# A recurrence with a router and experts on one core: w2 loaded into slots, in the order in which the first tiles need the experts

## The chip, the core and the metric

The kernel runs on one core of one Trainium2 chip. The metric is the device time of one launch in microseconds (us); lower is better. The engines are TensorE (PE, with PEld for its weight loads), VectorE (DVE), ScalarE (ACT), GpSimd (POOL) and SyncE (SP). Each works through its own queue in order. SP only issues transfers here, ACT and POOL issue some as well; all of them share 16 DMA engines.

## The reference

A gated linear recurrence over 4 x 8 heads of 768 steps and 48 channels gives 3072 rows of 384. A router takes two of eight experts for each row, and the row is the weighted sum of what these two compute.

```python
for t in range(S):
    state = alpha[:, :, t, :, None] * state + np.einsum('bhd,bhe->bhde', k[:, :, t], v[:, :, t])
    y[:, :, t] = np.einsum('bhd,bhde->bhe', q[:, :, t], state)
x = y.transpose(0, 2, 1, 3).reshape(B * S, H * D)            # 3072 x 384
noisy_logits = x @ w_gate + np.log1p(np.exp(x @ w_noise)) * noise
top2 = np.argpartition(-noisy_logits, 2, axis=1)[:, :2]      # two of 8 experts
top2_w = softmax over the two
for e in range(E):
    for k in range(2):
        mask = top2[:, k] == e
        h = np.maximum(x[mask] @ w1[e], 0.0)                 # 384 -> 1024
        out[mask] += top2_w[mask, k, None] * (h @ w2[e])     # 1024 -> 384
```

Everything is in float32. w1 and w2 are 8 x 1.5 MB each.

## The kernel before

The work has two stages, and one hand-written order (inside `tc.manual_schedule()`, from line 935) interleaves them on every engine.

**The recurrence** takes 24 chunks (NT) of 128 rows. `beside` is walked by n. Iteration n loads v of chunk n + 2 and alpha, k and q of chunk n + 4, updates the state, and then goes through a list of pieces in a fixed order: `alphas(n + 2)` (transposes on PE, then two scans on DVE, P_all and over, lines 286 and 292), `keys(n + 2)` (line 305 on POOL), `scores(n + 1)` and `give(n - 4)`, `queries(n + 2)` (q_P on DVE, line 314) and `masked(n + 1)` (line 333), router pieces, `turn_k`, `output(n)` (lines 210 and 214) and `turn_y(n - 1)`, which writes the rows to `x_rows` in DRAM. The transposes of one iteration share two PSUM buffers (`tp`). Three buffers (NIN) each hold the inputs alpha, k and q; they are tiles of their own (line 238), and their padding is set once on POOL.

**The router** works in units of three chunks (UC); there are 8 units (NU). `give(n - 4)`, four iterations after a unit's last chunk, calls `enter`, which ranks the unit's choices and queues six scatters of entries into `table` in DRAM (`put_some`, three per iteration, line 138), and `plan_tiles`, which lays out tiles of up to 128 rows of one expert. `GIVEN` says how many tiles are known after each unit. FULL = 23 tiles are planned from the first five units (u = 4, at n = 18), the other 32 from all eight (u = 7, at n = 27). For the units between, `plan_tiles` only copies. The plan has two columns per tile: the expert, and the tile's first row in `table`.

**The experts** take 51 tiles (ALWAYS), two per iteration from n = 23 (TILES_AT) on. Each has four steps (`tile_steps`): load w1 of tile i + 1, gather x of tile i + 2 and the first half of layer 1; its second half, then `combine(i - 1)`; transposes of tile i + 1 and the first half of layer 2; its second half, then `scale(i)` and `get_first(i)`. `load_tab(i + 4)` goes ahead of the first step: on SP for the first 23 tiles, on POOL for the others, waiting for the table entries of the units that the tile's plan knew. `get_first` gathers (on POOL) what an earlier tile wrote to the same output rows, `combine` adds on DVE, and a scatter on POOL puts the rows back. `get_first` waits for all scatters before it.

**w2** stays in SBUF, 98 KB per partition: `w2[:, e]` holds expert e. `load_w2(part)` loads a quarter of an expert (384 KB) on SP. The 32 quarters are spread over iterations 0 to 22, one or two each, in the order of the experts; layer 2 picks `w2[:, ds(e, 1)]` with a register that PE loads from the plan (line 793). w1 (1536 KB) is loaded per tile into two buffers, by a register that SP loads (line 746).

Of the kernel before, what the change touches and what calls it, by code (L numbers as in the profile page):

```python
# [9 lines left out]
F32 = mybir.dt.float32  # L10
U32 = mybir.dt.uint32
I32 = mybir.dt.int32
AF = mybir.ActivationFunctionType
ALU = mybir.AluOpType
# [4 lines left out]
def kernel(  # L19
# [26 lines left out]

    nc = tc.nc
    B, H, S, D = q.shape  # L50
    N, DM = out.shape
    E, _, F = moe_w1.shape
    C = 128
# [17 lines left out]
    TROWS = E * RMAX + (E + 0) * C  # L71
    NONE = 2 * N
    RANGE = 1e-18
    FULL = (2 * UT * (NU - 3) - E * (C - 1) + C - 1) // C
    GIVEN = [0] * (NU - 4) + [FULL, FULL, FULL, NTILE]

    def pool(name, bufs, on=ctx, **kw):
        return on.enter_context(tc.tile_pool(name=name, bufs=bufs, **kw))
# [104 lines left out]
    def turn_noise(by_chunk, on):  # L183
# [2 lines left out]
            nc.tensor.transpose(tp[:, e, :], by_chunk[:, e, :], ident[0:NT, 0:NT])  # L186
        nc.scalar.copy(noise.rearrange("p n e -> p e n"), tp)

    W2_PARTS = 4
    w2 = const.tile([C, E, FO, DM], F32, name="w2")  # L190

    def load_w2(part):
        e, f = divmod(part, W2_PARTS)
        fs = ds(f * FO // W2_PARTS, FO // W2_PARTS)
        nc.sync.dma_start(out=w2[:, e, fs], in_=moe_w2[e].rearrange("(a p) d -> p a d", p=C)[:, fs, :])


    def few(on, shape, name):
# [36 lines left out]

    def fast_gla(on):
        one, two = on["one"], on["two"]
        ins = {x: [one.tile([C, H, DP], F32, name=f"{x}_in{i}") for i in range(NIN)] for x in "akq"}
        for x in "akq":
            for t in ins[x]:  # L240
                nc.gpsimd.memset(t[:, :, D:DP], 1.0 if x == "a" else 0.0)
# [397 lines left out]
        del to_put[:n]  # L639


    plan = const.tile([C, NTILE, 2], I32, name="plan")
    given = const.tile([C, NTILE, EV], F32, name="given")
    so_far = [const.tile([C, EV], F32, name=f"so_far{i}") for i in range(2)]
    again = const.tile([1, 1], F32, name="again")
# [1 line left out]
    more = const.tile([1, 1], F32, name="more")  # L647
    more_i = const.tile([1, 1], I32, name="more_i")
    tiles_i = const.tile([1, 1], I32, name="tiles_i")

    def plan_tiles(u, on):
        rp = on["one"]
# [36 lines left out]
        def of_expert(dst, at, shape):  # L689
# [12 lines left out]
        nc.vector.tensor_scalar(out=start, in0=start, scalar1=0.0, scalar2=None, op0=ALU.max)  # L702
        nc.vector.tensor_tensor(start, start, ready, op=ALU.min)
        nc.vector.tensor_tensor(so_far[now % 2], start, old, op=ALU.add)

        behind = rp.tile([C, K_MAX, EV], F32, name="behind")[:, 0:K]
        nc.vector.tensor_tensor(behind, number, ends[:, None, :].to_broadcast(shape), op=ALU.is_ge)
# [5 lines left out]
        nc.vector.scalar_tensor_tensor(row, em, float(C), region[:, None, :].to_broadcast(shape), op0=ALU.mult,  # L713
                                       op1=ALU.add)
        nc.vector.tensor_mul(row, row, behind)
        first = rp.tile([C, K_MAX], F32, name="first")[:, 0:K]
        nc.vector.reduce_sum(out=first, in_=row, axis=mybir.AxisListType.X)
        nc.vector.tensor_scalar(out=plan[:, lo:hi, 1], in0=first, scalar1=float(TROWS - C), scalar2=None, op0=ALU.min)
# [4 lines left out]
    def experts(on):  # L723
# [10 lines left out]
        def load_tab(i, units):  # L734
            if i >= NTILE:
                return
            by, engine = (nc.sync, mybir.EngineType.SP) if i < FULL else (nc.gpsimd, mybir.EngineType.Pool)
            r = nc.values_load(plan[0:1, i, 1:2], engines=[engine], min_val=0, max_val=TROWS - C,
                               skip_runtime_bounds_check_because=WHY)
            tabs[i] = on["tab"].tile([C, 8], F32, name="tab")  # L740
            take_tile(by.dma_start(out=tabs[i][:, 0:4], in_=table.bitcast(F32)[ds(r, C), :]), units)
# [48 lines left out]
        def layer2(i, part):  # L790
            o = os_[i]
            if part == 0:
                o["e"] = nc.values_load(plan[0:1, i, 0:1], engines=[mybir.EngineType.PE], min_val=0, max_val=E - 1,
                                        skip_runtime_bounds_check_because=WHY)
                o["ps"] = on["o"].tile([C, DM], F32, name="o_ps")
            for f in range(FO // 2):
                fo = part * FO // 2 + f
                nc.tensor.matmul(o["ps"], o["h"][part][:, f, :],  # L798
                                 w2[:, ds(o["e"], 1), fo, :].rearrange("p o d -> p (o d)"),
                                 start=fo == 0, stop=fo == FO - 1)  # L800

# [106 lines left out]
    with ExitStack() as es:  # L910
# [9 lines left out]
        def steps_of(i, n):  # L920
            units = NU if n >= NT + 4 else unit_of[i] + 1
            limit = min(ALWAYS, GIVEN[units - 1])
            steps = tile_steps(i, do, (units, limit), i >= ALWAYS - 2)
            if i + 4 < limit:
                steps[0] = lambda go=steps[0]: (load_tab(i + 4, unit_of[i + 4] + 1), go())
            return steps


        TILES_AT = 23
        W2_ITERATIONS = 23  # L930
        held = []
        beside = [[] for n in range(TILES_AT)] + [list(range(i, min(i + 2, ALWAYS))) for i in range(0, ALWAYS, 2)]
        assert 2 * (NT + 4 - TILES_AT) + 4 <= FULL
# [1 line left out]
        with tc.manual_schedule():  # L935
            load(0)
            load_v(0)
            load(1)
            for n in range(2):
                alphas(n)  # L940
                keys(n)
                queries(n)
                load(n + 2) if n == 0 else (load_v(1), load(3))
            held.append(load_router(on))
            scores(0)
            masked(0)
            turn_k(0)
            for n, tiles in enumerate(beside):
                work = [step for i in tiles for step in steps_of(i, n)]
                w2_at = [E * W2_PARTS * min(i, W2_ITERATIONS) // W2_ITERATIONS for i in (n, n + 1)]  # L950
                w2_parts = lambda: [load_w2(i) for i in range(*w2_at)]
                chunk = [lambda: (load_v(n + 2), load(n + 4), state(n)), lambda: alphas(n + 2),
                         lambda: (keys(n + 2), choose_part(n - 2, 0), choose_part(n - 3, 2)),
                         lambda: (scores(n + 1), give(n - 4)), lambda: (queries(n + 2), masked(n + 1)),
                         lambda: (choose_part(n - 2, 1), choose_part(n - 3, 3), route(n - 1), w2_parts()),
                         lambda: turn_k(n + 1), lambda: output(n), lambda: turn_y(n - 1)]
                last = [lambda: put_some(UC)]
                if n == 1:
                    last.append(lambda: clear_table(on["two"]))
                if n == 2:  # L960
                    chunk.insert(1, lambda: turn_noise(held.pop(), on))
                if n == NT + 1:
                    chunk.insert(0, lambda: out_of_range(0))
                    last.append(lambda: out_of_range(1))

                some = range(4)
                if n == TILES_AT - 3:
                    last.append(lambda: [load_tab(i, unit_of[i] + 1) for i in some])
                if n == TILES_AT - 2:
                    chunk.insert(3, lambda: (load_w1(0), [gather_x(i, unit_of[i] + 1) for i in some[:2]]))  # L970
                if n == TILES_AT - 1:
                    chunk.append(lambda: turn_x(0))
                chunk += last
                done = 0
                for j in range(len(work)):
                    work[j]()
                    upto_j = len(chunk) * (j + 1) // len(work)
                    for piece in chunk[done:upto_j]:
                        piece()
                    done = upto_j  # L980
                for piece in chunk[done:]:
                    piece()
# [3 lines left out]
    with tc.If(any_more > 0):  # L986
# [3 lines left out]
                              skip_runtime_bounds_check_because="a count of at most 2 C rows")  # L990
        with tc.If(redo > 0):
            taken.clear()
            again_by_levels()


# [28 lines left out]
```

## Time and profile before

| | |
|---|---|
| time, three runs | 778.04 us median (776.23 to 783.17) |
| profiled run | 777.69 us, span of the trace 776.1 us, mean clock 0.991 |
| PE, matmuls | 744.0 us busy, 96% of the span |
| PEld | 613.3 us, 79% |
| DVE / ACT / POOL | 264.6 / 197.3 / 296.8 us |
| moved by DMA | 141.77 MB, 183 GB/s over the span |
| layer 1 (line 786), layer 2 (line 798) | 282.7 and 273.7 us of PE |
| chain that ended last | PE 71%, DVE 16%, issue 6%, DMA 3%, POOL 2% |

"Issue" is time in which an engine waited for nothing that the profile shows. Matmuls are pipelined and their ends are modelled, so that a busy PE need not be one at its peak. The profile's slices are a fortieth of the span, 19.4 us, and their digits tenths of busy time; PEclk is the clock that PE was granted. A wait is put down to the engine whose signal came last by the profile, and "x8" after an operation says how many instructions a line stands for. Idle time of an engine that doesn't bound anything costs nothing.

### The profile page before, as it was taken

Reading aid. Unit: us, or ns where it says so; the run is one execution under the profiler, and the core shown is the slowest. Engines: PE = TensorE matmul, PEld = TensorE weight load, DVE = VectorE, ACT = ScalarE, POOL = GpSimd, SP = SyncE. Lnnn points to the kernel's source line nnn. Section 1 sums busy time; section 2 is a strip of 40 time slices with the busy share of each in tenths; the row PEclk is TensorE's granted clock in tenths of the full one; section 3 lists DMA queues with packets and bytes.
Section 4 is the critical chain, followed back from the end, with each engine's and each line's share of the span. In section 5 each row is a group of like instructions: output and inputs, shape, how many; then the busy total and the mean of one; then the engine's idle time right before and its main releaser. Section 6 shows DMA issues by size and latency. Waiting matters only on the chain.

```text
span 776.1 us, 14314 instructions
## 1 busy us (share of the span) xinstructions
PE 744.0 (96%) x5239; PEld 613.3 (79%) x5239; DVE 264.6 (34%) x860; ACT 197.3 (25%) x381; POOL 296.8 (38%) x416
## 2 busy tenths in 40 slices
PE   5999999989899999989999999999999999999995
PEld 3988888878687888767788777887788877888774
DVE  6678998998302122301111111111111111111110
ACT  2456466545211221111111111111111111111110
POOL 4234666756523331333332333333333333333221
PEclk9999999999999999999999999999999999999998
DMA  9899999986834845365754565445544555455530
GB/s 152 156 217 197 186 199 189 206 190 180 266 106 161 268 159 186 109 210 154 252 187 190 213 219 181 156 176 196 189 174 149 203 205 210 169 177 214 208 123 23
DMA packets 149026, 141.77 MB, mean 183 GB/s; under 512 B 111725, under 2 KB 123599, under 8 KB 148948
## 3 DMA queue, kind: packets, MB, share of 16 engines
q1 hardware_dynamic: 135712, 116.45, 52.9%
q0 software_dynamic: 12224, 23.78, 9.4%
q8 instruction: 45, 0.74, 0.4%
q10 hardware_dynamic: 1012, 0.53, 0.3%
q14 instruction: 33, 0.27, 0.1%
HBM read 131.95 MB, written 15.25 MB: 190 GB/s over the span
## 4 chain that ended last, share of the span: by engine, by line
PE 71%; DVE 16%; issue 6%; DMA 3%; POOL 2%; ACT 0%; ACTq 0%; DVEq 0%; POOLq 0%
PE h_ps L786 31%; PE o_ps L798 30%; DVE over L292 3%; DVE P_all L286 3%; PE x_ps L775 2%; DVE MT L333 2%; PE tp L275 1%; PE o_ps L354 1%; DVE q_P L314 1%; PE y L214 1%; DMA prev<-out_dram,where 1%; PE sc L328 1%; PE y L210 1%; DMA x_in<-x_rows,where 1%; DMA out_dram<-prev,where 1%
## 5 line engine op out<-in xcount | busy, mean ns | idle before, releaser
L786 PEld LDWEIGHTS h_ps<-xt,w 128*128 128x128 f32 x2448 | 280.9, 192 | 15.7 <-DVE prev L819 3.1
L786 PE MATMUL h_ps<-xt,w 128*128 128x128 f32 x2448 | 282.7, 275 | 2.7 <-DVE prev L819 1.9
L798 PE MATMUL o_ps<-w,h 128*128 x816 | 273.7, 489 | 0.0
L798 PEld LDWEIGHTS o_ps<-w,h 128*128 128x128 f32 x816 | 151.7, 191 | 95.7 <-issue 2.1
L823 POOL DMA_INDIRECT out_dram<-prev,where x51 | 52.1, 1022 | 183.4 <-DVE prev L819 164.6
L788 ACT ACTIVATE h<-h_ps 128x512 f32<-128x512 f32 x102 | 61.0, 598 | 228.4 <-PE h_ps L786 220.5
L819 DVE SCALAR_TENSOR_TENSOR prev<-prev,tab,o 128x384 f32<-128x384 f32 x49 | 30.3, 618 | 256.7 <-DMA prev<-out_dram,where 144.3
L805 POOL DMA_INDIRECT prev<-out_dram,where x51 | 52.3, 1025 | 123.1 <-DMA out_dram<-prev,where 117.7
L777 DVE COPY xt<-x_ps 128x384 f32<-128x384 f32 x51 | 28.4, 557 | 181.4 <-PE x_ps L775 179.7
L814 ACT ACTIVATE o<-o_ps,tab 128x384 f32<-128x384 f32 x49 | 28.5, 581 | 234.7 <-PE o_ps L798 229.9
L766 POOL DMA_INDIRECT x_in<-x_rows,where x51 | 52.5, 1029 | 60.7 <-issue 45.5
L138 POOL DMA_INDIRECT table<-entry,place_u x48 | 50.5, 1051 | 13.4 <-issue 11.8
L305 POOL TENSOR_TENSOR k_P<-k_P,over 128x512 f32<-128x512 f32 x24 | 28.4, 1185 | 45.9 <-DVE over L292 32.7
L286 DVE TENSOR_TENSOR_SCAN P_all<-a_all,least 128x516 f32<-128x516 f32 x24 | 32.0, 1334 | 10.6 <-ACT a_all L283 5.2
L359 POOL TENSOR_TENSOR S<-S,end 128x384 f32<-128x384 f32 x20 | 22.7, 1135 | 32.7 <-DVE S L357 32.5
L292 DVE TENSOR_TENSOR_SCAN over<-a_all,P_all 128x515 f32<-128x515 f32 x24 | 34.1, 1421 | 0.8
L333 DVE COPY_PREDICATED MT<-upto,sc 128x512 f32<-128x512 uint32 x48 | 32.2, 723 | 1.3 <-PE sc L328 1.3
L328 PE MATMUL sc<-q_P,k_P 48*128 48x128 f32 x384 | 30.5, 297 | 1.2 <-DVE MT L333 0.9
L328 PEld LDWEIGHTS sc<-q_P,k_P 48*128 48x128 f32 x384 | 25.4, 198 | 5.9 <-issue 5.1
L775 PE MATMUL x_ps<-ident,x_in 128*128 128x128 f32 x153 | 25.1, 273 | 3.0 <-DMA x_in<-x_rows,where 3.0
L214 PE MATMUL y<-MT,vt 128*48 128x128 f32 x384 | 27.4, 287 | 0.0
L210 PE MATMUL y<-q_P,S 128*128 128x128 f32 x192 | 27.2, 287 | 0.0
(148 smaller groups left out, 600.8 us busy)
## 6 DMA issues: line engine op xcount, KB each, us to landing
w<-in_moe_w_dram SPq DMA_DIRECT2D x51, 1536.0 KB
w<-in_moe_w_dram SPq DMA_DIRECT2D x32, 384.0 KB
a_in<-in_alpha_dram SPq DMA_DIRECT2D x24, 192.0 KB
k_in<-in_k_dram SPq DMA_DIRECT2D x24, 192.0 KB
q_in<-in_q_dram SPq DMA_DIRECT2D x24, 192.0 KB
vt<-in_v_dram SPq DMA_DIRECT2D x24, 192.0 KB
x_rows<-y_sb SPq DMA_DIRECT2D x24, 192.0 KB
x_in<-x_rows,where POOLq DMA_INDIRECT x51
```

What stands on the lines that cost most here:

```text
L138: put = nc.gpsimd.indirect_dma_start(out=table, out_offset=bass.IndirectOffsetOnAxis(ap=place, axis=0), in_=entry, in_offset=None, bounds_ ...
L286: nc.vector.tensor_tensor_scan(P_all[:, 0:NP * CB], a_all[:, 0:NP * CB], least.rearrange("p j t -> p (j t)"), 0.0, op0=ALU.mult, op1=ALU.max)
L292: nc.vector.tensor_tensor_scan(over.rearrange("p j t -> p (j t)")[:, :0:-1], a_all[:, :1:-1], P_all[:, :1:-1], 0.0, op0=ALU.mult, op1=ALU.max)
L328: nc.tensor.matmul(c["sc"][i][:, j, :], c["k"][r, j, :], c["q"][r, j, :], start=True, stop=True)
L333: nc.vector.copy_predicated(MTs[n % 2][:, i], mask_upto, sc)
L766: nc.gpsimd.indirect_dma_start(out=x_in[i % NB], out_offset=None, in_=x_rows[0:units * UT, :], in_offset=bass.IndirectOffsetOnAxis(ap=wher ...
L775: nc.tensor.transpose(x_ps[:, a, :], x_in[i % NB][:, ds(a * C, C)], ident)
L786: nc.tensor.matmul(h_ps[:, fo, :], w1[:, a, ds((part * FO // 2 + fo) * C, C)], xt[:, a, :], start=a == 0, stop=a == KO - 1)
L788: nc.scalar.activation(os_[i]["h"][part], h_ps, AF.Relu)
L798: nc.tensor.matmul(o["ps"], o["h"][part][:, f, :], w2[:, ds(o["e"], 1), fo, :].rearrange("p o d -> p (o d)"), start=fo == 0, stop=fo == FO ...
L805: get = nc.gpsimd.indirect_dma_start(out=prev[i % 2].bitcast(U32), out_offset=None, in_=out.bitcast(U32), in_offset=bass.IndirectOffsetOnA ...
L823: put = nc.gpsimd.indirect_dma_start(out=out, out_offset=bass.IndirectOffsetOnAxis(ap=where[:, 0:1], axis=0), in_=rows, in_offset=None, bo ...
```

## The change

There are five parts.

1. w2 becomes eight slots. Slot k holds the k-th expert of those that the first batch of tiles uses (in the order of their number, and the unused ones behind them). `order_slots`, new, works this out on DVE right after the first plan; `expert_in` says which expert is in a slot, `slot_of` where an expert is. `load_w2` reads `expert_in` into an SP register for every quarter, and the plan gets a third column, the slot, which PE's register takes in layer 2.
2. The first batch is planned from four units: FULL is 17, planned at u = 3 (n = 15), and the second batch, at n = 27, has 38 tiles.
3. The w2 loads start at n = 16: one quarter at each of n = 16 to 19, four at 20, four at 21, one at 22 (after the router pieces, as before), and then two after the second and two after the fourth step of each tile, until all 32 are out: 19 quarters in tiles 0 to 4.
4. Tile i is declared free of the loads of slots behind i (up to i = 6), since the tiles before it use at most one new slot each.
5. The nine input tiles of alpha, k and q lie in the last one and a half slots of w2 instead of tiles of their own.

`load_tab` still issues on SP for tiles 0 to 22 (ALWAYS - 28 = 23).

```diff
-    FULL = (2 * UT * (NU - 3) - E * (C - 1) + C - 1) // C
-    GIVEN = [0] * (NU - 4) + [FULL, FULL, FULL, NTILE]
+    FULL = (2 * UT * (NU - 4) - E * (C - 1) + C - 1) // C
+    GIVEN = [0] * (NU - 5) + [FULL, FULL, FULL, FULL, NTILE]
...
     def load_w2(part):
-        e, f = divmod(part, W2_PARTS)
+        k, f = divmod(part, W2_PARTS)
         fs = ds(f * FO // W2_PARTS, FO // W2_PARTS)
-        nc.sync.dma_start(out=w2[:, e, fs], in_=moe_w2[e].rearrange("(a p) d -> p a d", p=C)[:, fs, :])
+        e = nc.values_load(expert_in[0:1, k:k + 1], engines=[mybir.EngineType.SP], min_val=0, max_val=E - 1,
+                           skip_runtime_bounds_check_because="a permutation of the experts")
+        put = nc.sync.dma_start(out=w2[:, k, fs],
+                                in_=moe_w2[ds(e, 1)].rearrange("o (a p) d -> p (o a) d", p=C)[:, fs, :])
+        for take in w2_takes:
+            tc.declare_no_dep(put.ins, take, reason="a slot behind those that the tile may take")
+        w2_loads[k].append(put.ins)
+
+    def take_w2(i, take):
+        for loads in w2_loads[i + 1:] if i < E - 1 else []:
...
-        ins = {x: [one.tile([C, H, DP], F32, name=f"{x}_in{i}") for i in range(NIN)] for x in "akq"}
+        places = w2.rearrange("p e f d -> p (e f d)").rearrange("p (n h d) -> p n h d", h=H, d=DP)
+        ins = {x: [places[:, E * FO * DM // (H * DP) - 1 - i - NIN * "akq".index(x)] for i in range(NIN)] for x in "akq"}
...
+    def order_slots(tiles, rp):
+        used = rp.tile([C, E], F32, name="used")
+        nc.vector.tensor_scalar(out=used, in0=tiles[:, 0:E], scalar1=1.0, scalar2=None, op0=ALU.min)
+        upto_it = rp.tile([C, E], F32, name="upto_it")
+        nc.vector.tensor_tensor_scan(upto_it, ones[:, 0:E], used, 0.0, op0=ALU.mult, op1=ALU.add)
+        nc.vector.memset(slot_of, 0.0)
+        nc.vector.tensor_tensor(slot_of[:, 0:E], upto_it, used, op=ALU.subtract)
...
+        nc.vector.tensor_copy(out=expert_in, in_=used)
...
+        if u is not None and not lo:
+            order_slots(so_far[now % 2], rp)
...
+        nc.vector.tensor_tensor(slots, behind, slot_of[:, None, :].to_broadcast(shape), op=ALU.mult)
+        slot = rp.tile([C, K_MAX], F32, name="slot")[:, 0:K]
+        nc.vector.reduce_sum(out=slot, in_=slots, axis=mybir.AxisListType.X)
+        nc.vector.tensor_copy(out=plan[:, lo:hi, 2], in_=slot)
...
-            by, engine = (nc.sync, mybir.EngineType.SP) if i < FULL else (nc.gpsimd, mybir.EngineType.Pool)
+            by, engine = (nc.sync, mybir.EngineType.SP) if i < ALWAYS - 28 else (nc.gpsimd, mybir.EngineType.Pool)
...
-                o["e"] = nc.values_load(plan[0:1, i, 0:1], engines=[mybir.EngineType.PE], min_val=0, max_val=E - 1,
+                o["e"] = nc.values_load(plan[0:1, i, 2:3], engines=[mybir.EngineType.PE], min_val=0, max_val=E - 1,
...
+            for at in (1, 3):
+                steps[at] = lambda go=steps[at]: (go(), more_w2(2))
...
-        W2_ITERATIONS = 23
+        w2_beside = {TILES_AT - n: parts for n, parts in ((7, 1), (6, 1), (5, 1), (4, 1), (3, 4), (2, 4), (1, 1))}
+        w2_parts = iter(range(E * W2_PARTS))
...
-                         lambda: (choose_part(n - 2, 1), choose_part(n - 3, 3), route(n - 1), w2_parts()),
+                         lambda: (choose_part(n - 2, 1), choose_part(n - 3, 3), route(n - 1), more_w2(w2_beside.get(n, 0))),
```

Left out: seven more instructions of `order_slots`, the column count of the plan, and lines for a general path that this input doesn't take.

## The prediction

> **What bounds the kernel now.** I read the page's slices first, then table of stretches, waits, timelines. The slices (19.4 us each) show two stages: ten with VectorE (DVE) and the DMA engines full, then thirty in which only TensorE (PE) is.
>
> ```profile
> PE   5999999989899999989999999999999999999995
> DVE  6678998998302122301111111111111111111110
> PEclk9999999999999999999999999999999999999998
> DMA  9899999986834845365754565445544555455530
> ```
>
> The same by stretches: us, busy time of PE, weight loads, DVE, ACT, POOL, then clock, DMA share, GB/s.
>
> ```profile
> 20.00:190.00 170.00, 162.99 (x1655) 147.06 (x1655) 146.75 (x350) 92.45 (x201) 92.19 (x145) 0.99 0.92 189
> 190.00:255.00 65.00, 61.48 (x423) 50.90 (x422) 17.07 (x81) 14.51 (x28) 26.91 (x35) 0.97 0.58 183
> 255.00:345.00 90.00, 86.88 (x517) 68.16 (x516) 23.38 (x118) 16.65 (x28) 28.28 (x32) 0.98 0.53 182
> 345.00:740.00 395.00, 395.00 (x2455) 318.69 (x2454) 60.92 (x289) 64.67 (x110) 133.58 (x142) 1.00 0.54 191
> ```
>
> In the recurrence (20 to 190 us) DMA is 0.92 busy, but PE is idle for only 7.0 us of 170; from 190 to 345 it is idle 6.6 us, from 345 to 740 not at all. A tile of the experts is a fixed 10.85 us (h_ps from 431.08 to 441.93). All that a change off PE can win before the tail is about 14 us of idle time, plus what the clock lost.
>
> In the chain of waits one full iteration of the recurrence on PE, back to back, is scores 1.09, q transposes 0.59, logits 0.80, turned keys 0.48, y 0.89 and 1.01, turned y 0.59, state 0.87, a and k transposes 0.87: 7.19 us. The P_all scans on DVE start at 66.12, 74.21, 82.12, 89.99, 97.88 and so on to 156.46, 169.38, 178.24, 185.03: 118.9 us for 15 iterations. PE's own share is 15 x 7.19, less 2 x (0.87 + 0.48) for chunks without a state: 105.2. The excess is 13.7, of which 12.92 - 7.19 = 5.7 is the iteration that plans tiles (n = 18). Here is what it does on DVE, and what PE does meanwhile and later:
>
> ```profile
> 159.76 0.98 DVE L629 SCALAR_TENSOR_TENSOR place_u<-at_f,place_f 128x6 uint32<-128x6 f32 x1
> 160.68 0.15 DVE L667 COPY total_sb<-h_ps 128x8 f32<-128x8 f32 x1
> 166.92 0.26 DVE L720 TENSOR_SCALAR given<-given 128x207 f32<-128x207 f32 x1
> 167.09 0.68 DVE L314 TENSOR_TENSOR q_P<-tp,P_all 128x512 f32<-128x512 f32 x1
> ```
>
> ```profile
> 159.55 1.07 PE L232 MATMUL h_ps<-w_r,yT 128*128 128x16 f32 x8 [1.07 <-DVE picked L622]
> 161.12 1.91 PE L210 MATMUL y<-q_P,S 128*128 128x128 f32 x8
> 336.83 0.55 PE L775 MATMUL x_ps<-ident,x_in 128*128 128x128 f32 x3 [2.99 <-DMA x_in<-x_rows,where]
> 337.35 7.12 PE L798 MATMUL o_ps<-w,h 128*128 x16
> ```
>
> The plan holds q_P back from 160.7 to 167.1. After a short PE idle y takes 1.91 instead of 1.06 us and o_ps 7.12 instead of 5.33: windows of 1 us show the granted clock at 0.50 from 161 to 164 and from 195 to 198. The one later stall, 2.99 us, follows the second plan (DVE 306.5 to 314.1).
>
> Does DMA bound anything? The SyncE (SP) queue in mid-recurrence:
>
> ```profile
> 120.31 1.25 SPq L163 DMA_DIRECT2D a_in<-in_alpha_dram  x1
> 121.61 5.20 SPq L163 DMA_DIRECT2D k_in<-in_k_dram  x1
> 126.85 1.00 SPq L163 DMA_DIRECT2D q_in<-in_q_dram  x1
> 127.89 1.16 SPq L195 DMA_DIRECT2D w<-in_moe_w_dram  x1
> ```
>
> PE's waits for it up to 190 us (total, times, longest):
>
> ```profile
> PE tp L275 <- DMA a_in<-in_alpha_dram: 5.4, 2, 4.2
> ```
>
> SP issues without a pause from 76 to 165 us, and one issue takes up to 5.20 us where the quick ones take 0.4[...]. Yet of the 5.4 us that PE waited for a_in, 4.2 is the first load, before any w2. The rest is 1.2, and DVE waits 1.68 before P_all at 178.24 with no cause named, perhaps q_in. The loads run four chunks ahead, so full rings cost almost nothing yet.
>
> **What the Trainium skill says.** "DMA: Bandwidth & Descriptors", section "Issuing engines are not separate DMA queues": all issuers run on the same 16 engines and interleave. The trace agrees: in the tiles the gather of prev (issued 203.22) lands at 212.06, in and ahead of a burst of w1. "TensorE: Matmul & The Clock Gate", Part 1: PE's clock halves after an idle window of about 3.4 us and stays so for at least one. The half rates seen here last about 3.4 us; that about 1 us of idle is enough is this trace's, not the page's.
>
> **The change part by part.**
>
> *Removed from the recurrence:* w2's 32 loads of 384 KB, 1.4 per iteration up to n = 22. Now 13 go out at n = 16 to 22 (8 of them at 20 and 21, where no a, k or q is loaded any more), 19 beside tiles 0 to 4. Gain: the 1.2 and 1.68 us of waits, 2.9. Bounds: 0 (those waits have other causes) and 8.0 (all of 13.7 - 5.7 is lost to DMA). I take 2.9.
>
> *Added to DVE at n = 15:* order_slots, 13 small instructions and a memset. Small dependent ones start 0.20 apart (161.64, 161.84, 162.06, 162.26): 13 x 0.20 + 0.06 = 2.7 us. The plan moves from n = 18 to 15 with 17 tiles for 23: 153 elements for 207 are 54/0.96 = 0.056 us less (the slope of 0.38 at 207 and 0.46 at 288 is 0.0010 per element) in 11 instructions, -0.6. Three new ones (slots, slot, the plan's third column): 0.32 + 0.32 + 0.18 = 0.8. Net 2.7 - 0.6 + 0.8 = 2.9. It stands before q_P and masked on DVE; PE's turned y waits for q_P's PSUM buffer, and next iteration's P_all and POOL's k_P follow. DVE is busy 146.75 of 170, PE 162.99: no slack to absorb it, so 2.9 in full. Bounds: 1 (slack of the two lighter iterations, 16 and 17) and 2.9 + 1.7 (another half-clock window of 3.4 us).
>
> *Second plan (n = 27):* 38 tiles for 32. 54 elements more in 11 instructions is +0.6, three new at 342 elements 0.52 + 0.52 + 0.18: +1.8 together. In the chain behind it (x_in, put, prev, table puts, x_in again at 329.32, landing before 336.83) everything shifts, so the 2.99 us stall becomes 4.8. I take 1.8; bounds 0 and 3.5 (a second half-clock window).
>
> *Moved to the tiles:* 4 x 384 KB per tile, beside w1's 1536 KB, so twice the bytes. A w1 burst takes about 4 us (568 to 573, up to 414 GB/s); w2's will take as much. Bursts of two w1 already occur (207 to 216, 230 to 238, 254 to 262) and only the first ends in a PE idle, 1.90 us at 212.87. SP holds w2 behind w1(i+1), and w1(i+2) behind it: 8 of 10.85 us. w1(3), issued 229.87, is needed at 238.55, and w1(4), issued 232.89, at 250.93, so 4 us more hidden. Slot loads: slot 3 is complete in tile 0, 4 in tile 1, ..., each three tiles before a tile can wait for it. Cost -1.9 (that idle disappears) to +10 (rival C), taken 0.5.
>
> *SP:* each w2 load gets a register load. Four tab issues with theirs took 3.27 us, 0.8 each, so four w2 loads are 3 to 4 us of a 7 us iteration at n = 20 and 21; x_rows (n - 1) and the four tab loads are behind them, then w1(0) at 188.85, needed at 199.82: hidden. expert_in is ready at n = 15, so n = 16 doesn't wait. *load_tab* keeps its first 23 on SP; 17 to 22 now wait for the last table puts (350.25), with w1(14) behind them: about 355 to 359, needed at 366.0. 0, bounds 0 and 3. *Inputs inside w2* and the third plan column read by PE: same instructions, nothing.
>
> Sum: -2.9 + 2.9 + 1.8 + 0.5 = +2.3. The profiled span 776.1 becomes 778.4. Its run took 777.69, close to the median 778.04 of 776.23 to 783.17; so 780.3, said as 780.
>
> **Rivals.**
>
> A, above: 780, own range 776 to 786.
>
> B, DMA was the hidden bound: SP's unbroken queue speaks for it, the short waits for a_in against. Then all 8.0 of excess go, with the 1.90 at 212.87, the 0.92 idle at 192 and its half-clock (1.7): -12.5, +2.9 + 1.8: -7.8, 770 (765 to 774).
>
> C, ends slower: the chain put, prev, combine falls behind in tiles 0 to 4. get_first(i) waits on POOL for the put before to land, then combine waits on DVE for prev, and xt of the tile after next stands behind combine. With one w1 burst per tile the chain's cycle, when catching up, is 8.4 us (prev at 360.98, 369.28, 377.69). If w2's burst adds its whole 3.9 us it is 12.3, over 10.85: 1.5 late per tile, 7 after five, met at n = 27 by the longer plan: 7 + 1.7 of clock + 2.3 - 0.5, about +10.5, so 789 (785 to 795). It decides from 10.85 us on. Against it: the double bursts above.
>
> D, the change doesn't do what it says: the input tiles, now part of w2, make loads wait for each other or slots for inputs. Price, if each chunk's three loads land one after another at 2 us each, some 4 us in part of 20 iterations: +20 and more, 800. Against: three w2 loads left in 1.6 us at 189 to 192 into one tile without waiting.
>
> **How the numbers follow.** A 0.53, B 0.20, C 0.22, D 0.05. The predicted time is A's. Under 1%, 7.8 us, a measurement of this kernel can hardly tell from no change (its own runs spread 6.9). Faster by over 1% is below 770.3: 0.14, all from B. Slower, above 785.8: most of C (0.18), D 0.05, A's end 0.03: 0.26. Within: 0.60. The range 769 to 792 leaves out some of B's and C's ends (0.06 and 0.07) and D.
>
> **What would show it.** DVE at n = 15 some 9 us between place_u and q_P, none at n = 18 (plan right). P_all iterations at n = 6 to 13 still 7.0 to 8.2 us with DMA well below 0.9: A; all near 7.2: B. SP issues near 0.4 us and pauses in SP's queue. Tiles 0 to 5 at 10.85 us plus recurrence work: A; growing idle before h_ps with prev or x_in as releaser: C. PE idle near 337 of 4.8 us. Wrong altogether if PE's own time per tile or iteration changed, or SP waited on w2.

## The result, and the profile after

The changed kernel takes 787.25 us (median of four runs, 786.08 to 789.54) against 778.04 before: a ratio of 1.0114 with an interval of 1.0069 to 1.0160, so it is slower by about 1%. The profiled span grew from 776.1 to 784.4 us, by 8.3, and the mean clock fell from 0.991 to 0.984.

The slices of the page after (19.6 us each) show the same two stages. New are a dip of PE and of its clock in the eighth slice, and DMA that is less full before that slice and fuller behind it.

```profile
PE   5999999799989999989999999999999999999995
DVE  6779999879411121510111111111111111111110
PEclk9999999699999999999999999999999999999998
DMA  9777678388979765446665544555544555445530
```

The stretches after, as before: us, busy time of PE, weight loads, DVE, ACT, POOL, then clock, DMA share, GB/s.

```profile
20.00:190.00 170.00, 161.52 (x1606) 145.76 (x1606) 146.16 (x350) 90.87 (x198) 89.25 (x143) 0.96 0.73 136
190.00:255.00 65.00, 60.45 (x424) 50.05 (x425) 21.03 (x94) 14.16 (x29) 24.59 (x32) 0.97 0.87 295
255.00:345.00 90.00, 85.97 (x532) 69.61 (x531) 23.96 (x114) 17.08 (x29) 31.07 (x35) 0.98 0.58 186
345.00:740.00 395.00, 394.03 (x2427) 316.51 (x2426) 61.78 (x296) 64.51 (x109) 135.05 (x144) 1.00 0.54 191
```

The transfers did move: in the recurrence the DMA share fell from 0.92 to 0.73, and in the next 65 us it rose from 0.58 to 0.87. PE didn't profit. In the recurrence it is busy 1.5 us less out of 170, at a clock of 0.96 where it was 0.99.

The loss can be located from the start of the scores on PE in each iteration. The intervals between these starts, in the same order before and after, are:

```
n = 6 to 13  before  8.10 7.32 7.91 8.45 6.29 7.19 8.04 7.19
             after   8.14 7.32 7.91 8.46 6.29 7.19 8.04 7.18
n = 14 to 21 before  7.91  8.45  6.29 7.20 12.50 7.70 8.03 7.75
             after   7.30 15.86 11.12 7.19  7.74 7.19 7.29 7.96
```

Interval n runs from the scores issued in iteration n to those of n + 1. The plan stands behind the scores of its iteration: it makes the 12.50 of before (n = 18) and the 15.86 of after (n = 15). This is the sum, by the starts of scores, of the first half of layer 1 of each tile, and of the end:

| us later (+) or earlier (-) than before | |
|---|---|
| first scores and the two intervals behind them | -1.1 |
| three iterations without a plan (7.91, 7.70, 8.03 become 7.30, 7.19, 7.29) | -1.9 |
| the plan's own iteration: +7.41 at n = 15, -4.76 at n = 18 | +2.65 |
| the iteration behind the plan at n = 15: 6.29 becomes 11.12 | +4.83 |
| the last interval, 7.75 becomes 7.96 | +0.2 |
| tile 0: 13.05 becomes 13.82; tile 4: 10.85 becomes 12.10 | +2.0 |
| tiles 9 to 11, the second plan: 10.95, 11.06, 16.08 become 11.20, 13.89, 14.01 | +1.0 |
| other tiles and the end | +0.6 |
| sum | +8.3 |

DVE in the plan's iteration after, cut to the ends of its three parts. `used` opens `order_slots`, `expert_in` closes it, q_P is what waits.

```profile
136.64 0.98 DVE L648 SCALAR_TENSOR_TENSOR place_u<-at_f,place_f 128x6 uint32<-128x6 f32 x1
...
141.42 0.17 DVE L673 TENSOR_SCALAR used<-so_far 128x8 f32<-128x8 f32 x1
...
143.76 0.17 DVE L690 CAST expert_in<-used 128x8 int32<-128x8 f32 x1
...
146.79 0.68 DVE L333 TENSOR_TENSOR q_P<-tp,P_all 128x512 f32<-128x512 f32 x1
```

From total_sb (137.56) to q_P the plan holds DVE for 9.2 us where it held it for 6.4. `order_slots` takes 2.42 us of it (141.42 to 143.84).

PE in the same stretch and later, each line with its idle time in brackets:

```profile
136.42 1.07 PE L249 MATMUL h_ps<-w_r,yT 128*128 128x16 f32 x8 [1.62 <-DVE picked L641]
...
148.25 2.58 PE L347 MATMUL sc<-q_P,k_P 48*128 48x128 f32 x16 [3.55 <-DVE MT L352]
...
153.24 2.05 PE L227 MATMUL y<-q_P,S 128*128 128x128 f32 x8
...
218.34 2.92 PE L834 MATMUL h_ps<-xt,w 128*128 128x128 f32 x24 [2.71 <-DMA w<-in_moe_w_dram]
...
338.10 7.25 PE L834 MATMUL h_ps<-xt,w 128*128 128x128 f32 x48 [2.78 <-DVE xt L825]
346.33 0.55 PE L823 MATMUL x_ps<-ident,x_in 128*128 128x128 f32 x3 [0.97 <-DMA x_in<-x_rows,where]
```

PE stops for 3.55 us ahead of the scores of iteration 16: they wait for DVE, where q_P and the masking MT stand behind the plan. These scores then take 2.58 us instead of 1.09, and the y behind them 2.05 instead of 1.06. That is the clock. The windows of this stretch (columns as in the stretches above) show it at half speed for the 10 us after the stop, with PE busy all the time; in the third window DMA moves almost nothing:

```profile
142.00:148.70 6.70, 2.43 (x19) 1.88 (x17) 6.22 (x26) 3.87 (x8) 0.04 (x1) 0.98 0.82 145
148.70:152.00 3.30, 3.30 (x22) 3.02 (x21) 3.23 (x6) 0.00 (x0) 1.68 (x1) 0.50 0.48 125
152.00:158.70 6.70, 6.70 (x39) 6.07 (x39) 3.52 (x16) 1.21 (x3) 4.98 (x7) 0.51 0.02 1
158.70:164.00 5.30, 5.30 (x60) 4.81 (x60) 4.29 (x6) 3.94 (x9) 1.49 (x4) 1.00 0.56 122
```

A shorter stretch at half speed, 3.41 us behind the ranking's stop, lies in the plan's iteration of both kernels (160.72 to 164.13 before, 138.15 to 141.56 after), so it doesn't count in the difference.

SP's queue is no longer continuous: here it pauses from 120.68 to 123.97. The issues of alpha and k, which took 1.25 and 5.20 us in the lines shown of before, take 0.71 and 1.11.

```profile
117.64 0.71 SPq L164 DMA_DIRECT2D w<-in_alpha_dram  x1
118.41 1.11 SPq L164 DMA_DIRECT2D w<-in_k_dram  x1
119.56 1.12 SPq L164 DMA_DIRECT2D w<-in_q_dram  x1
123.97 0.34 SPq L244 DMA_DIRECT2D x_rows<-y_sb  x1
```

### The profile page after: what moved, and what is told of

It reads as the page before. It is cut to its first block, busy times and chain, and to the rows that moved or that the text cites. A ratio compares the mean times of both kernels' runs of the same rounds, so it can differ in the third digit from the quotient of the medians.

```text
span 784.4 us, 14445 instructions
## 1 busy us (share of the span) xinstructions
PE 747.8 (95%) x5239; PEld 617.5 (79%) x5239; DVE 270.0 (34%) x878; ACT 196.8 (25%) x381; POOL 297.3 (38%) x416
## 4 chain that ended last, share of the span: by engine, by line
PE 71%; DVE 14%; issue 6%; DMA 5%; POOL 2%; ACT 1%; ACTq 0%; SPq 0%; POOLq 0%; DVEq 0%
PE h_ps L834 30%; PE o_ps L846 28%; DVE over L311 3%; DMA w<-in_moe_w_dram 3%; DVE P_all L305 2%; PE tp L294 2%; PE x_ps L823 2%; PE y L231 2%; PE sc L347 2%; DVE MT L352 2%; PE y L227 1%; PE o_ps L373 1%; PE h_ps L249 1%; PE tp L241 1%; DMA out_dram<-prev,where 1%
## 5 line engine op out<-in xcount | busy, mean ns | idle before, releaser
L139 POOL DMA_INDIRECT table<-entry,place_u x48 | 52.1, 1086 | 13.4 <-issue 11.6
L294 PE MATMUL tp<-ident,w 128*128 128x128 f32 x288 | 46.1, 298 | 7.2 <-DMA w<-in_alpha_dram 5.3
L294 PEld LDWEIGHTS tp<-ident,w 128*128 128x128 f32 x288 | 35.5, 156 | 11.8 <-POOL w L260 4.2
L311 DVE TENSOR_TENSOR_SCAN over<-a_all,P_all 128x515 f32<-128x515 f32 x24 | 36.4, 1517 | 0.8
```

The costliest lines, as they stand in the source:

```text
L139: put = nc.gpsimd.indirect_dma_start(out=table, out_offset=bass.IndirectOffsetOnAxis(ap=place, axis=0), in_=entry, in_offset=None, bounds_ ...
L294: nc.tensor.transpose(tp[:, j, :], src[:, 2 * j:2 * j + 2, :], ident)
L311: nc.vector.tensor_tensor_scan(over.rearrange("p j t -> p (j t)")[:, :0:-1], a_all[:, :1:-1], P_all[:, :1:-1], 0.0, op0=ALU.mult, op1=ALU.max)
```

## The experiments

All are timed in five rounds against the kernel before on the same chip. There were four sets, and the kernel before is not equally fast in them: 785.4 us in the first (e1 to e4), 777.1 in the second (e0, e5, e6, e7), 785.3 in the third (e8, e9), 783.8 in the fourth (e10, e11). The chip alone doesn't decide it: the second and the fourth set ran on the same one. So only ratios, and times within a set, are compared. "After" and "before" are the two kernels of the study.

**e0: the changed kernel again**

> The changed kernel as it is, beside the kernel before on the same chip as the other runs of this set: ratio 1.007 to 1.016, and in its trace the 9 us plan at n = 15 with the half clock behind it.

Measured: 786.02 us against 777.07, ratio 1.0128 (1.0098 to 1.0159). The plan's iteration and the next are 15.86 and 11.12 us, as in the first trace. Tiles 0 and 4 are not as there: 12.37 and 11.62 us, together 0.1 us over the kernel before, where the first trace has 2.0. That row of the table above isn't steady.

**e1: the order of the slots left out**

```diff
+    nc.vector.memset(slot_of, 0.0)
+    nc.vector.tensor_copy(out=slot_of[:, 0:E], in_=expert_ids)
+    nc.vector.tensor_copy(out=expert_in, in_=expert_ids)
...
-        if u is not None and not lo:
-            order_slots(so_far[now % 2], rp)
```

The slots are fixed by the experts' numbers at the start; for this input that is the order which `order_slots` would find.

> The changed kernel without order_slots: slot k holds expert k, set once at the start (for these inputs the first 17 tiles use experts 0 to 6 in the order of their number, so it is the same order). Theory H (the plan at n = 15 holds q_P and masked on DVE, PE runs idle, and its clock halves for 10 us): 2.4 us of DVE less, the 3.55 us idle of PE before the scores shrinks to about 1, the half clock at n = 16 to one window of 3.4 us or none: 5 to 7 us less than the changed kernel, 780 to 782 us. Theory L (the w2 loads beside the tiles are the loss: w1 and prev land late): at most the 2.4 us, about 785 us, and the waits for w1 in tiles 1 and 5 stay.

Measured: 787.92 us, ratio 1.0017 (0.9995 to 1.0038). Its trace has 13.31 and 10.11 for the plan's iteration and the next: shorter by 2.55 and 1.0 than in the first trace of after, and by 2.0 and nothing than in e10's (15.32 and 10.10), which is the same kernel as after. So 2.4 us of small DVE work left out shorten the plan's iteration by about as much. The half clock was expected to shrink to 3.4 us or to none; it lasts 6.8 us, as long as in e10 (0.50 from 152 to 158).

**e2: the kernel before with the early plan alone**

```diff
-    FULL = (2 * UT * (NU - 3) - E * (C - 1) + C - 1) // C
-    GIVEN = [0] * (NU - 4) + [FULL, FULL, FULL, NTILE]
+    FULL = (2 * UT * (NU - 4) - E * (C - 1) + C - 1) // C
+    GIVEN = [0] * (NU - 5) + [FULL, FULL, FULL, FULL, NTILE]
```

> The kernel before with one part of the change alone: the first batch of 17 tiles planned from four units at n = 15, the second of 38 at n = 27; w2 and inputs as before. Theory H: the hold is about 5.5 us instead of 6.4, so the first plan costs no more than at n = 18; the longer second plan adds about 0.5: 777 to 779 us. If the place n = 15 itself costs (it is followed by two iterations without slack), 781 to 783. Theory L: as before, 778.

Measured: 783.69 us, ratio 0.9976 (0.9956 to 0.9996). To plan at n = 15 instead of 18, without `order_slots` and with w2 loaded as before, costs nothing in this set. (Not shown in the edit: `load_tab` keeps its first 23 on SP, and two scratch tiles share a place.) In its trace PE waits 1.88 us for k_in at 135.43, ahead of the plan; the iterations are 10.16 and 13.59, and the one behind the plan is 6.29.

**e3: the w2 loads alone**

The fixed slots of e1, and the plan of before (five units, 23 tiles, at n = 18); the w2 loads as in the changed kernel.

```diff
-    FULL = (2 * UT * (NU - 4) - E * (C - 1) + C - 1) // C
-    GIVEN = [0] * (NU - 5) + [FULL, FULL, FULL, FULL, NTILE]
+    FULL = (2 * UT * (NU - 3) - E * (C - 1) + C - 1) // C
+    GIVEN = [0] * (NU - 4) + [FULL, FULL, FULL, NTILE]
```

> The changed kernel with fixed slots (as in e1) and the plan of before (23 tiles from five units at n = 18, 32 at n = 27): the move of the w2 loads and of the inputs alone. Theory H: the relief of the recurrence (2.4 us less by n = 15) against 2.0 us more waiting for w1 in tiles 1 and 5: 777 to 779 us. Theory L: 783 to 786 us, most of the loss is here.

Measured: 786.72 us, ratio 1.0013 (0.9994 to 1.0031). Moving w2 away from the recurrence brings nothing that can be measured. The iterations ahead of the plan are those of the trace of before (7.92, 8.45, 6.29, 7.19), and the two behind it, n = 19 and 20, take 7.64 and 7.82 us, where e9 below, with the same plan and w2 loaded as before, has 7.19 and 7.20. So shorter iterations outside the plan can't be put down to w2's move. PE waits 2.98 us for w1 in tile 0.

**e4: spare work on PE ahead of the waiting scores**

```diff
+        def keep_busy(times):
+            bank = on["h"].tile([C, FO // 2, C], F32, name="h_ps")
+            for t in range(times):
+                nc.tensor.transpose(bank[:, t % 4, :], ident, ident)
...
+                if n == 16:
+                    chunk.insert(3, lambda: keep_busy(24))
```

> The changed kernel with 24 spare transposes of the identity on PE (0.147 us each, 3.5 us together) ahead of the scores of n = 16, where PE waits 3.55 us; nothing uses their result. Theory H: PE's clock isn't halved from 148 to 158 us, the iteration after the plan takes about 7 us instead of 11.1: 4 us less than the changed kernel, 783 us. If DVE's backlog alone sets that iteration, the clock doesn't matter: 787 us, or up to 2 more. Theory L says nothing here: 787.

Measured: 789.54 us, ratio 1.0054 (1.0032 to 1.0076). The plan's iteration stays at 15.89 us, the next falls to 6.79. PE's timeline, with the spare transposes in the first line:

```profile
145.73 2.78 PE L994 MATMUL h_ps<-ident 128*128 128x128 f32 x24
149.46 1.67 PE L347 MATMUL sc<-q_P,k_P 48*128 48x128 f32 x16 [0.94 <-DVE MT L352]
...
152.36 1.14 PE L227 MATMUL y<-q_P,S 128*128 128x128 f32 x8
...
218.14 4.39 PE L834 MATMUL h_ps<-xt,w 128*128 128x128 f32 x24 [4.76 <-DMA w<-in_moe_w_dram]
```

y takes 1.14 us, not 2.05, and the clock is 1.00 in every window from 144 to 164. The stop itself is as long as ever, since q_P comes no earlier; only what follows it is faster. Part of the gain is waited away again: PE stops 4.76 us for w1 in tile 0 (last line), where it stops 2.05 us in e1 and 2.98 in e3. In this set the changed kernel itself wasn't timed, hence e10 and e11.

**e10 and e11: the same comparison on one chip**

> The changed kernel itself, as the measure for e11 on the same chip. The iteration of the plan 15.9 us and the next 11.1, as in its first profile; ratio to the kernel before 1.005 to 1.013, the lower end if this chip is one on which the kernel before takes 785 rather than 777.

> The changed kernel with the 24 spare transposes of e4 ahead of the scores that wait for the plan. If 4.3 us of the loss are PE's halved clock after its stop of 3.6 us, the iteration after the plan is 6.8 us, not 11.1, and the median lies 4 us (0.5%) below e10's. If the 4.3 us are a wait of the chain behind the plan that the clock only goes along with, or come back as a later stop, the two medians are equal within 1 us.

Measured: e10, the changed kernel, 788.99 us, ratio 1.0073 (1.0051 to 1.0095); e11, with the transposes, 787.57, ratio 1.0067 (1.0043 to 1.0091). The windows of e10 and then of e11, over the scores behind the plan and the next iteration (the clock is the third column from the end):

```profile
148.50:152.00 3.50, 3.43 (x27) 3.13 (x27) 3.43 (x5) 0.99 (x2) 1.68 (x1) 0.76 1.22 206
152.00:158.00 6.00, 5.79 (x35) 4.95 (x35) 3.70 (x17) 1.26 (x4) 4.83 (x7) 0.57 0.01 1
```

```profile
149.00:152.00 3.00, 3.00 (x33) 2.88 (x32) 2.93 (x5) 0.17 (x1) 1.68 (x1) 1.00 0.43 131
152.00:158.00 6.00, 5.87 (x64) 5.04 (x63) 5.62 (x20) 4.28 (x8) 5.08 (x7) 1.00 0.39 75
```

In the same 6 us e11 does 64 PE instructions and e10 35. The plan's iteration is 15.32 us in both, the next 10.10 in e10 and 6.80 in e11: 3.3 us, all from the clock, and still there at the last scores (196.08 against 192.83) and the first tile (205.30 against 202.21). But the medians lie only 1.4 us apart, and their intervals overlap. The traces are of quick runs: e11's is the fastest of its 22 (782.09), e10's the third fastest of 17 (786.45). The mean clock of all runs says that the transposes act in the usual run too: its median is 0.981 in e10 and 0.987 in e11, and 0.006 of 788 us are 4.7 us, by this estimate some 9 us less at half speed. So the place and the size of the clock's part are shown in the traces; that the whole of it reaches the time of a run is not. The 4 us that were expected of the median didn't come, and where the usual run loses them again was not found.

**e5: w2 kept out of tile 0**

```diff
-        w2_beside = {TILES_AT - n: parts for n, parts in ((7, 1), (6, 1), (5, 1), (4, 1), (3, 4), (2, 4), (1, 1))}
+        w2_beside = {TILES_AT - n: parts for n, parts in ((7, 2), (6, 2), (5, 2), (4, 2), (3, 4), (2, 1))}
...
-                steps[at] = lambda go=steps[at]: (go(), more_w2(2))
+                steps[at] = lambda go=steps[at], parts=(2 if at == 1 else 1) if i else 0: (go(), more_w2(parts))
```

> The changed kernel with w2's loads kept away from the first w1 loads: two quarters at n = 16 to 19, four at 20, one at 21, none at 22, none in tile 0, then three per tile instead of four. Theory L (w2 in front of w1 makes it late): PE's wait ahead of tile 1 (2.7 us in the changed kernel, 1.9 before) goes below 1, tile 5's goes too: 2 to 4 us less than the changed kernel. Theory S (w1 of tile 1 is late because of the scatters of table entries and the gathers before and beside it, which are the same in the kernel before): that wait stays at 2 to 3 us, tile 5's goes: about 1 us less.

Measured: 785.76 us, ratio 1.0120 (1.0090 to 1.0149), e0 of the same set 786.02. Tile 0 is 10.95 us where e0 has 12.37: the wait for w1(1) is gone, which fits w2's transfers as what delayed w1. It doesn't settle it: in e2 and e8, with w2 loaded as before, PE stops 3.65 and 3.20 us for w1 at the same place. Tile 4 still waits 1.23 us, now with three quarters per tile. The gain of 1.4 us is too small for the median to tell.

**e6: the changed kernel with its plans in pieces**

Both plans become generators that stop every four instructions or so (about 1 us); two pieces go into each iteration from n = 15, the rest into n = 20, the second plan's into n = 27 and 28. The w2 loads begin two iterations later (2, 2, 4, 4, 1).

```diff
+                planned = UC * (GIVEN.index(FULL) + 1) + 3
+                if planned <= n < TILES_AT - 3:
+                    chunk.insert(5, lambda: plan_some(1))
+                    chunk.insert(8, lambda: plan_some(1))
+                elif n in (NT + 3, NT + 4):
+                    for at in (5, 6, 7, 8, 9, 10, 11):
+                        chunk.insert(at, lambda: plan_some(1))
+                else:
+                    chunk.insert(4, lambda: plan_some(99))
```

> The changed kernel with both plans cut into pieces of about 1 us of DVE: the first (with order_slots) in two pieces per iteration from n = 15 to 19 and its rest at 20, the second over the pieces of n = 27 and 28; the w2 loads then start at n = 18 (2, 2, 4, 4, 1). Theory H: no PE idle of over 1 us and no half clock behind the plans, so the plan costs what DVE has no slack for, about 4 of its 9 us, and nothing of the half clock (4.8): 8 to 11 us less than the changed kernel, ratio 0.997 to 1.002 to the kernel before. If it is DVE's work alone that costs: 2 to 3 us less.

Measured: 777.20 us, ratio 0.9999 (0.9984 to 1.0014), e0 of the same set 786.02. The time is that of the kernel before again, but the trace (of the second slowest of the 22 runs) doesn't show the loss of the first plan taken back. What it shows is the second plan: tiles 9 to 11 take 32.55 us, and 39.38 in e0, so 6.8 less. In the recurrence n = 15 and 16 fall to 12.69 and 6.30 us, but the pieces lengthen n = 18 to 20 to 9.06, 8.22 and 11.61. From n = 14 to 21 it takes 70.1 us in all; e0 takes 71.6, e10 70.1, the kernel before 65.8. PE still stops, by the ranking at n = 15 and where the rest of the plan holds q_P at n = 20:

```profile
137.28 1.89 PE L249 MATMUL h_ps<-w_r,yT 128*128 128x16 f32 x8 [1.72 <-DVE picked L648]
...
184.81 1.11 PE L241 MATMUL tp<-ident,yT 128*128 128x128 f32 x4 [2.84 <-DVE q_P L333]
```

The clock is halved for 6.8 us around the first stop and for 3.4 around the second. So the expected end of stops and half clock came at the second plan alone, and the ratio of 1.00 is the sum of a loss that stays and a gain that the kernel before can have as well (e9). 1.54 us for w1 in tile 4 remain, too.

**e7: the kernel before with the early plan and both plans in pieces**

The edits of e2 and e6 on the kernel before, w2 loaded as there.

> The kernel before with the early plan (as in e2) and both plans cut into the same pieces: w2 and inputs as before. Theory H: the 5.7 us of the first plan shrink to 1 or 2, the stall and the half clock behind the second (about 5 us) go: 8 to 9 us less than the kernel before, ratio 0.987 to 0.991. If DVE's work alone costs: ratio 0.997.

Measured: 771.72 us (770.11 to 773.12), ratio 0.9935 (0.9910 to 0.9959): faster than both kernels. Two iterations are still long, 11.29 and 11.48 us, each with a stop and the half clock behind it; n = 14 to 21 take 66.0 us together, as in the kernel before (65.8), so in this trace (of the slowest of its 8 runs) the pieces of the first plan gain nothing. The first, from PE's timeline:

```profile
137.00 0.29 PE L672 MATMUL h_ps<-seen,ones 128*128 128x8 f32 x2
138.99 1.06 PE L232 MATMUL h_ps<-w_r,yT 128*128 128x16 f32 x8 [1.71 <-DVE picked L629]
140.38 1.69 PE L210 MATMUL y<-q_P,S 128*128 128x128 f32 x8
```

The plan's sum over the rows (first line) takes one of the PSUM buffers that the logits need, beside the ranking's: the logits wait until DVE has read the ranking's.

**e8: the first plan's pieces one iteration later**

The edit against e7:

```diff
-                if planned <= n < TILES_AT - 3:
-                    chunk.insert(5, lambda: plan_some(1))
-                    chunk.insert(8, lambda: plan_some(1))
+                if 15 <= n < TILES_AT - 3:
+                    a, b = ((0, 0), (2, 1), (2, 1), (0, 0), (1, 1))[n - 15]
+                    chunk.insert(5, lambda: plan_some(a))
+                    chunk.insert(8, lambda: plan_some(b))
```

> The kernel before with both plans cut into pieces, the first begun one iteration later than in e7 (three pieces each in n=16 and 17, none in n=15 and 18 where entries are ranked, two in n=19, the rest in n=20). If PE's stop of 1.7 us in n=15 came from the plan's sum taking a PSUM buffer behind the ranking, and the one of 2.1 us in n=18 from pieces beside the ranking's DVE work, the iterations of 11.3 and 11.5 us fall to 7.2 to 8.5, the clock stays near 1.00, and 4 to 7 us of e7 go: ratio to the kernel before 0.985 to 0.990. If the plan's work costs what it costs wherever it lies, a stop and a halved clock come elsewhere: ratio 0.992 to 0.995 as in e7.

Measured: 777.06 us against 785.33, ratio 0.9913 (0.9882 to 0.9944). The gain hoped for didn't show. The stop for the ranking is gone from n = 15, but in this set PE waits 2.01 us for v (at 135.90) just there, so that the iterations are 9.96 and 12.19, and n = 18 stays at 10.79 with a stop of 1.12. Whether the later start helps where the loads are in time is left open.

**e9: the second plan alone in pieces**

On the kernel before; the first plan whole, at n = 18. The generator is that of e6, not shown.

```diff
-                plan_tiles(n // UC, on)
+                todo.append(plan_steps(n // UC, on))
...
+                if n in (NT + 3, NT + 4):
+                    for at in (5, 6, 7, 8, 9, 10, 11):
+                        chunk.insert(at, lambda: plan_some(1))
+                else:
+                    chunk.insert(4, lambda: plan_some(99))
```

> The kernel before with the second plan alone cut into seven pieces in each of the iterations 27 and 28; the first plan stays whole and late. If e7 won by the second plan, tiles 10 and 11 are 10.85 us each as there, 5 us less than before, and the ratio is 0.993 to 0.994, the same as e7's. If half of e7's gain came from the first plan, 0.996 to 0.997.

Measured: 777.13 us, ratio 0.9918 (0.9892 to 0.9943), the same as e8 in its set and as e7 within the intervals. PE's timeline where the kernel before stopped for 2.99 us and then had half the clock for 3.4 us:

```profile
331.30 5.33 PE L816 MATMUL o_ps<-w,h 128*128 x16
336.46 5.52 PE L804 MATMUL h_ps<-xt,w 128*128 128x128 f32 x48
341.82 0.49 PE L793 MATMUL x_ps<-ident,x_in 128*128 128x128 f32 x3
342.15 5.33 PE L816 MATMUL o_ps<-w,h 128*128 x16
```

No stop, and no o_ps of 7.12 us. Tiles 9 to 11 take 32.5 us instead of 38.1 in the trace of before: 5.6 us, against a gain of 6.4 (0.0082 of 785). So the second plan alone accounts for e7's gain.

This trace also shows a likely reason for the kernel before taking 7 to 8 us more in three of the sets than in one:

```profile
135.52 1.09 PE L275 MATMUL tp<-ident,k_in 128*128 128x128 f32 x4 [2.32 <-DMA k_in<-in_k_dram]
136.54 2.08 PE L328 MATMUL sc<-q_P,k_P 48*128 48x128 f32 x16
...
142.76 1.91 PE L210 MATMUL y<-q_P,S 128*128 128x128 f32 x8
```

One wait of 2.32 us for k, and scores and y take double their time behind it: the two iterations are 11.08 and 11.91 us where the trace of before has 7.91 and 8.45, 6.6 us more. e2 and e8, which load w2 as before, have such a wait at the same place (1.88 us for k, 2.01 for v). e1, e3, e4, e10 and e11, which load w2 later, have none in those sets.

## Why the prediction came out as it did

The forecast was 780 us (769 to 792), and within 1% the likeliest; it came out at 787.25: slower by just over 1%, the side that was given 0.26, and outside A's own range of 776 to 786. That it still lies within 769 to 792 is luck, since the upper end of that range stood for C, whose mechanism didn't occur (below). The forecast sum was +2.3 us, the span grew by 8.3. Taken by the steps of the sum:

- **"Added to DVE at n = 15 ... I take 2.9 in full": right.** DVE's hold was put at some 9 us and measured 9.2; `order_slots` at 2.7 and measured 2.42; the plan's own iterations cost +2.65 net.
- **"Bounds ... 2.9 + 1.7 (another half-clock window of 3.4 us)": this is the step that failed.** I put 0 for the clock into the sum and 1.7 as its worst case. The iteration behind the plan, at half speed, became 4.83 us longer. My bound held one window of 3.4 us, because the half rates of the trace before lasted about that long; this one lasted 10 us. The Trainium skill, "TensorE: Matmul & The Clock Gate", Part 1, reckons the loss as half of the throttled time; half of 10 us is 5.0, and the trace agrees with its 4.83. e4 (11.12 becomes 6.79) and e11 against e10 (10.10 becomes 6.80) show that it is the clock and not a wait, by 4.3 us in the one pair and 3.3 in the other; a median gave back 1.4 us, not clear of noise, so what the clock costs a usual run stays open.
- **The gain for w2's loads removed from the recurrence, "I take 2.9": measured 1.9, and not shown to be w2's.** Of my two waits the 1.2 us for a_in was never w2's. It lies at 8.88 us, among the first loads, and is still there after (1.07 us at 8.75). I booked it without asking where in time it lies. The 1.68 us before P_all are gone after, but in e9 too, which loads w2 as before. The short iterations don't follow w2 either: n = 14 is 7.29 in e7, with w2 as before, and 7.91 in e1, with w2 moved; n = 19 and 20 are 7.19 and 7.20 in e9, and 7.64 and 7.82 in e3, with w2 moved.
- **w2 beside the tiles, "taken 0.5": measured 2.0 in the first trace, 0.1 in e0's.** In the first, tile 0 waits 2.71 us for w1(1) in place of 1.90 for prev, and tile 4 1.09 for w1(5). That the first is w2's doing is likely by e5, not shown.
- **The second plan, "I take 1.8": measured 1.0.** The stop became 2.78 and 0.97 us, not 4.8 in one piece.

The terms of the sum gave +2.3; with the measured ones it is -1.9 + 2.65 + 4.83 + 2.0 + 1.0 = +8.6, and the start, 1.1 us earlier by chance, with +0.8 of remainders brings it to the span's +8.3. The clock's term, 0 in the forecast, is the largest of them.

The rivals. **D** falls: the iterations keep their length, and the inputs are loaded four chunks ahead as before. **C** falls as a mechanism: the time that it named, 789, was near, but no tile grows through the chain of put, prev and combine; the two waits of tiles 0 to 4 are for w1. **B** falls for the trace of before: with DMA at 0.73 instead of 0.92, the iterations n = 6 to 13 agree within 0.04 us. For the other sets it is half right. There the kernel before has times of 784 to 785 us, kernels with its loads show a wait for an input with a halved clock behind it, and the changed kernel's ratio is 1.0073, not 1.0128. That the relief makes this difference is argued from traces of e2, e8 and e9; the kernel before itself was not traced in those sets. Even there the relief is less than what the plan and the tiles cost.

**A** was right in two things, that DMA doesn't bound in the trace of before and that the plan's DVE work goes in full onto PE's path. It left out PE's clock. e6 doesn't confirm the rest of it, although its ratio is 0.9999: its gain lies at the second plan. Its fair partner is e7, with the same pieces and w2 loaded as before, in the same set: 771.72 us against 777.20. Of the traces' difference (777.3 and 771.5) 4.1 us lie in n = 14 to 21 and 2.8 in tiles 0 and 4, less 1.8 at the start. So some 5 us stay lost even with the plans in pieces. The two differ in how w2 is loaded and in `order_slots`, and these were not separated.

## What to carry to other kernels

A few us of serial work on a second engine are to be priced twice where PE has no slack: as the stop, and as the halved clock that can follow it. In these traces the clock (3.3 and 4.3 us) cost more than the added work (2.65); in medians that much was not seen. A long plan is best cut into pieces of about 1 us where the engine that runs it has time to spare: e9's change of one place, among the tiles, is worth 0.8%, while moving 12 MB of loads was worth nothing. In the recurrence, where DVE is busy 147 of 170 us, the pieces only moved the stops (e6, e7). A ratio of 1.00 doesn't say that a loss is gone; look in the trace for the place where the time came back. A DMA share of 0.92 isn't a bound so long as iterations keep PE's own length, and it pays to look up where in time a wait lies before it is booked as relief.

## What the runs showed of the hardware

- Every stretch at half clock that lies within one of these traces lasted 3.41, 6.83 or 10.24 us: one, two or three times the same length. The stop ahead of it doesn't decide which. 1.07 and 2.99 us (the kernel before, 159.55 and 336.83) were followed by 3.41, 1.88 us (e2, 135.43) and 3.55 us (after) by 10.24. A stop of 1.08 us at the same place was followed by 6.83 in e10 and by none in e11. What does decide was not found.
- In after, PE was busy through all of the 10.24 us. The Trainium skill, "TensorE: Matmul & The Clock Gate", Part 1, has what is issued in the first 3.4 us or so run at half speed and everything after it at full speed; here it took three times that, and the measurement decides.
- 24 transposes of a constant, 2.78 us of PE, ahead of the stop kept the clock at 1.00 in both traces that have them (e4, e11); PE's stop was then 0.94 and 1.09 us, where it was 3.55 (after) and 1.94 (e10).
- The same kernel before takes 777 us in one set and 784 to 785 in three others, on one and the same chip in two of them. Three kernels that load w2 as it does show one input about 2 us late in the slower sets, with the clock halved for 10.24 us behind it in each (e2, e8, e9).
